# A gated mix of sliding-window and recurrent memory attention: tail products moved into the sliding branch's last block, and one ring of streamed weight slices for tail and steps

## The chip, the cores and the metric

The kernel runs on one core of one Trainium2 chip. The metric is device time in microseconds (us), the median over runs. Engines: PE (TensorE) multiplies, DVE (VectorE), ACT (ScalarE) and POOL (GpSimd) do the rest, SP (SyncE) only issues transfers; POOL issues some as well. "PEld" is PE loading weights. The granted clock is the share of PE's full clock that the chip allowed.

## The reference, cut to what matters

Two branches on the same input, mixed by a gate:

```
x = A_x; g = sigmoid(sum(x * gate_w))                    # one gate per token
# A: causal attention over a window of 256, 32 heads of 20, 2048 tokens, width 640
a = A(x, wqkv, wo)
# B: 64 segments of 32 tokens, 32 heads of 192, with 8 memory tokens ahead of each
mem = mem0
for s in range(64):
    h = concat([mem, x[32*s : 32*s+32]])                 # 40 tokens
    q, k, v = h @ Wq, h @ Wk, h @ Wv                     # 640 -> 32 x 192 each
    p = softmax(mask(q @ k.T * 192**-0.5))               # memory rows see all keys
    o = (p @ v) @ Wo                                     # 32 x 192 -> 640
    mem, b[s] = o[:8], o[8:]
out = g * a + (1 - g) * b
```

Branch B is serial: a segment's memory is an output of the segment before. `branch_A` therefore prepares the input for B as well.

## The kernel before, in words

Four stages follow each other.

1. **Sliding branch** (`branch_A`), 16 blocks of 128 queries, 32 heads each. A loop over n (block and head) emits, per pair of heads, scores by query (PSUM banks "s", L327), their row maximum on DVE (L357), and 22 heads later scores by key ("st") with the exponential on ACT (L387) and a mask on POOL (L395); eight heads after that come the values (L411). Between them stand units from a list: the next block's preparation (transposes, Q, K and V products in banks "m") and the projection of the block before (L435, L445). For the last block there is no next block to prepare. Transposed input goes to DRAM for branch B (`xa_dram`), and the last eight tokens of each segment into `xTb` (its *tail* tokens). A list `units` holds SP's work for branch B: 21 weight slices are packed into DRAM (`w_packed`) and 23 resident weight tiles are loaded (`early`). A unit is taken when n is divisible by a number that grows as the list gets shorter; what is left at the end is added without any condition.
2. **Tail.** The 24 tokens of a segment that are not its tail tokens go through the steps together with the 8 memory tokens, 32 columns at a time. The Q, K and V of the tail tokens depend on no memory, so they are made in advance for all segments, per group g of eight heads: `tail_qk` (L590; four blocks of six products, 20 matmuls each) and `tail_v` (L610), written to DRAM as `xbqk` and `xbv`. Q and K of group 0 are added at the end of the sliding branch, with banks "s"; the rest is `tail_projections`: V of group 0, the initial memory turned by PE (L640) and copied to `m0T`, Q and K of groups 1 to 3, V of groups 1 to 3. The remaining resident weights (`late`) are loaded on SP here. Streamed slices come through a ring `t_w` of three.
3. **Steps** (`branch_B`), 64 of them, in the order of the string `STEP`. q, k, v are products of the 32-column `hT` with weight slices (L775); scores (L847), softmax, transposed probabilities (L896), values (L921) and the output projection (L945) follow for each of four groups. The output projection ends a step: DVE writes its memory columns into the next `hT` (L956), and the next step's products wait for that. Of the weights, 21 slices a step are streamed from `w_packed` through a ring of five (L754 on SP); the others are resident. `last`, two o tiles of group 3, are loaded during step 0, four issues of 80 KB each (L532).
4. **Mix** (`mix_out`): gate and sum, to the output.

The order on each engine is fixed ahead by a planner (`Sched`). It keeps, per buffer tag, the rule that a buffer is written only after the users of the one that held its slot, gives each operation a duration and a latency, and takes the ready operation with the longest chain behind it. On PE it does that in the sliding branch only; in tail and steps PE keeps the order in which operations were made. SP and POOL execute their queues in the planned order: an issue that waits holds all behind it.

For the first step, `load_x(0)` brings `hT` from `xa_dram` on POOL (L732) and DVE copies `m0T` into it (L762); both belong to `branch_B`. The rings of tail and steps are separate pools, and the steps' pools take the memory that the tail's pools gave back:

```
shape = {"ts": (2, [P, P // MEM, 2, 12, MEM]), "w": (3, [P, WQ]), "m0": (1, [P, D])}   # tail
"w": (5, [P, WQ]), "hT": (1, [P, KT, SEG]), ...                                         # steps
early, late, last = weights.resident[:23], weights.resident[23:-2], weights.resident[-2:]
```

Of the kernel before, what the change touches and what calls it, by code (L numbers as in the profile page):

```python
# [139 lines left out]
def branch_A(tc, x, wqkv, wo, gate_w, spread_x, ga_dram, omg_dram, units, tail, W=256, HA=32):  # L140
# [13 lines left out]
    with ExitStack() as ctx:  # L154
# [307 lines left out]
        for _, u in prep_units(0):  # L462
            u()
        queue, credit, share = [], 0.0, 0.0
        job = lambda n: divmod(n, HA) if 0 <= n < HA * NB else None
        for n in range(HA * NB + LAG2):
            t, h = divmod(n, HA)
            if h == 0:
                if t + 1 < NB:
                    queue += prep_units(t + 1)  # L470
                credit, share = 0.0, sum(c for c, _ in queue) / (HA - 3)
            if n >= HA and units and n % max(1, HA * (NB - 2) // (len(units) + 1)) == 0:
                units.pop(0)(sc, [o for o in sc.ops[-8:] if o["eng"] == "PE"][-1:])
# [12 lines left out]
            while queue and credit > 0 and n % BURST == BURST - 1:  # L486
                c, u = queue.pop(0)
                credit -= c
                u()
        for u in units:  # L490
            u(sc, [])
        for _, u in queue:
            u()
        tail(sc)
        with tc.manual_schedule():
# [6 lines left out]
WQ, WO = 4 * 384, 2 * D  # L502
PARTS = {"q": KT, "k": KT, "v": KT, "o": 6}


# [69 lines left out]

def tail_qk(sc, nc, weights, xTb, xbqk, g, loads, after=(), tag="m"):

    HS = P // MEM
    ws = tail_weights(sc, nc, weights, g, "qk", loads)
    for t in range(xbqk.shape[2] // HS):  # L580
        st = sc.buf("ts")
        for n in range(6):
            kind, b4 = "qk"[n // 3], n % 3
            ps, use = sc.buf(tag), [ws[kind, g, kt] for kt in range(KT)]

            def f(ps=ps, use=use, b4=b4, t=t):
                for bb in range(4):
                    c = (4 * b4 + bb) * P
                    for kt in range(KT):
# [3 lines left out]
            evacuate(sc, nc, n, ps, st, lambda st=st, n=n, b4=b4: sc.tile(st)[:, :, n // 3, 4 * b4:4 * b4 + 4, :].rearrange("p s b t -> p b s t"),  # L593
                     lambda ps=ps: sc.tile(ps)[:].rearrange("p (b s t) -> p b s t", b=4, t=MEM))
        sc.op("POOL", 1000, lambda st=st, t=t: nc.gpsimd.dma_start(xbqk[g, :, t * HS:(t + 1) * HS].rearrange("p s k c -> p (s k c)"),
                                                                 sc.tile(st)[:].rearrange("p s k b t -> p (s k b t)")), reads=[st])


# [18 lines left out]

def tail_projections(tc, weights, xTb, xbqk, xbv, post, late, mem0, m0T, ident):

    nc = tc.nc  # L620
    with ExitStack() as ctx:
        shape = {"ts": (2, [P, P // MEM, 2, 12, MEM]), "w": (3, [P, WQ]), "m0": (1, [P, D])}
        pools = {t: ctx.enter_context(tc.tile_pool(name=f"t_{t}", bufs=n)) for t, (n, _) in shape.items()}
        pools["m"] = ctx.enter_context(tc.tile_pool(name="t_ps", bufs=8, space=bass.MemoryType.PSUM))

        def make(tag, n):
            if tag == "m":
                return pools[tag].tile([P, 512], FP32, name="t_psum", tag=tag)
            return pools[tag].tile(shape[tag][1], BF, name=f"t_{tag}", tag=tag)
        sc = Sched({"ts": 2, "w": 3, "m": 8, "m0": 1}, make)  # L630
        loads = {}
        for n, u in enumerate(late):
            loads[u] = sc.op("SP", 1300, lambda u=u: weights.load_resident(post, u, nc.sync), after=[loads[late[n - 1]]] if n else [])
        tail_v(sc, nc, weights, xTb, xbv, 0, loads)
        m0, tp = sc.buf("m0"), sc.buf("m")
        view = lambda: sc.tile(tp)[:].bitcast(BF)[:, 0:KT * MEM].rearrange("p (k t) -> p k t", k=KT)

        def turn_m0():
            for kt in range(KT):
                nc.tensor.transpose(view()[:, kt, :], sc.tile(m0)[0:MEM, kt * P:(kt + 1) * P], ident[0:MEM, 0:MEM])  # L640
        sc.op("DMA", 500, lambda: nc.gpsimd.dma_start(sc.tile(m0)[0:MEM], mem0), writes=[m0])
        sc.op("PE", 300, turn_m0, reads=[m0], writes=[tp], name=("m0",), mode=128)
        sc.op("DVE", dve_ns(40), lambda: nc.vector.tensor_copy(m0T[:], view()), reads=[tp])
        for g in range(1, 4):
            tail_qk(sc, nc, weights, xTb, xbqk, g, loads)
        for g in range(1, 4):
            tail_v(sc, nc, weights, xTb, xbv, g, loads)
        with tc.manual_schedule():
            sc.run()
# [4 lines left out]

KEPT = {"QT": (1, [P, 12 * L + 64 - L]), "Kz": (1, [P, 4, 2, L]), "Px": (1, [P, P])}

# [35 lines left out]

def branch_B(ctx, tc, xa_dram, xbqk, xbv, m0T, constants, weights, xo_dram, last):
    nc = tc.nc
# [5 lines left out]
    sb = {  # L700
        "w": (5, [P, WQ]), "hT": (1, [P, KT, SEG]), "tok": (2, [P, 384]), "vtok": (1, [P, 384]), "K02": (1, [P, 4, 2, L]),
        "PTm": (1, [P, 2, 4, L]), "PTx": (1, [P, 2, 4, L]), "OT": (1, [P, 3, 4, L]), "Pm": (1, [P, 4, SEG]),
        "xqk": (2, [P, 2, 12, MEM]), "xv": (1, [P, 384]), "oT": (1, [P, KT, SEG]),
    }
    ps = {"mm": 3, "tr": 2, "s": 2, "o": 1}
    pools = {t: ctx.enter_context(tc.tile_pool(name=f"b_{t}", bufs=n)) for t, (n, _) in sb.items()}
    pools |= {t: ctx.enter_context(tc.tile_pool(name=f"b_ps_{t}", bufs=n, space=bass.MemoryType.PSUM)) for t, n in ps.items()}
    stats = ctx.enter_context(tc.tile_pool(name="b_stats", bufs=3))
    sc = Sched({t: n for t, (n, _) in sb.items()} | {t: n for t, (n, _) in kept.items()} | ps)

    def tile_of(b, shape=None, dtype=BF, name=None):
        t = b["tag"]
        if b["tile"] is None:
            if t in kept:
                b["tile"] = still[t][b["n"] % kept[t][0]]
            elif t in sb:
                b["tile"] = pools[t].tile(sb[t][1], BF, name=f"t_{t}", tag=t)
            else:
                b["tile"] = pools[t].tile(shape, dtype, name=name or f"p_{t}", tag=t)
# [40 lines left out]

    hts = {0: load_x(0)}
    sc.op("DVE", dve(40), lambda: nc.vector.tensor_copy(tile_of(hts[0][0])[:, :, 0:MEM], m0T[:]), writes=[hts[0][0]], after=[hts[0][1]])  # L762
    made, tails, loads = {}, {}, {}
# [251 lines left out]
def kernel(  # L1015
# [32 lines left out]
    weights = Weights(nc, dram, B_Wq, B_Wk, B_Wv, B_Wo, streamed)  # L1048
    early, late, last = weights.resident[:23], weights.resident[23:-2], weights.resident[-2:]
    pre = ctx.enter_context(tc.tile_pool(name="b_pre", bufs=1))  # L1050
# [7 lines left out]
    with tc.tile_pool(name="b_xtail", bufs=1) as xtail:  # L1058
        xTb = xtail.tile([P, KT, nseg * MEM], BF, name="xTb")

        def spread_x(sc, qb, xT):
# [3 lines left out]
            for i in range(n):  # L1065
# [8 lines left out]
        branch_A(tc, x, A_wqkv, A_wo, gate_w, spread_x, ga_dram[:], omg_dram[:], units,  # L1074
                 lambda sc: tail_qk(sc, nc, weights, xTb, xbqk, 0, packs, xTb_ops[-1:], "s"))
        const = ctx.enter_context(tc.tile_pool(name="b_const", bufs=1, side="right"))
        constants = constants_B(nc, const)
        m0T = const.tile([P, KT, MEM], BF, name="m0T")
        post = ctx.enter_context(tc.tile_pool(name="b_post", bufs=1, side="right"))
        tail_projections(tc, weights, xTb, xbqk, xbv, post, late, mem0, m0T, constants[1])  # L1080

    with ExitStack() as inner:
        end = inner.enter_context(tc.tile_pool(name="b_end", bufs=1))
        branch_B(inner, tc, xa_dram, xbqk, xbv, m0T, constants, weights, xo_dram, {u: lambda u=u: weights.load_resident(end, u, nc.sync) for u in last})
    mix_out(tc, xo_dram, omg_dram[:], ga_dram[:], outf)
# [35 lines left out]
```

## Time and profile before

| | us |
|---|---|
| median of 7 runs | 2268.62 |
| lowest and highest run | 2260.5, 2283.53 |
| profiled execution, its time | 2268.62 |
| its span, first to last instruction | 2266.9 |

| stage of the profiled execution | from, to (us) | PE busy, us of stage | granted clock | DMA, GB/s |
|---|---|---|---|---|
| sliding branch to the first L590 | 0, 360 | 337.17 of 360 | 0.98 | 80 |
| L590 of group 0 and the branch's end | 360, 400.5 | 39.86 of 40.5 | 0.98 | 69 |
| tail | 400.5, 541 | 136.16 of 140.5 | 0.98 | 243 |
| step 0 | 541, 578 | 26.37 of 37 | 0.94 | 284 |
| steps 1 to 62 | 578, 2205.5 | 1496.80 of 1627.5 | 0.98 | 307 |
| step 63 and mix | 2205.5, 2267 | 35.18 of 61.5 | 0.72 | 246 |

"Busy" of PE is the time in which some matmul is under way; matmuls overlap, so a busy PE may still run at half clock. The chain of waits follows the work that ended last back to its releasers; the table of PE's waits counts the time in which PE stood still, by what ended it. The two can differ: the chain names a transfer even when PE had other work until just before it landed.

### The profile page before, as it was taken

How to read it: one execution, taken by the hardware profiler on the slowest of the kernel's cores; microseconds unless marked ns; L12 is line 12 of the kernel's file. 1: busy time of each engine (PE TensorE's matmuls, PEld its weight loads, DVE VectorE, ACT ScalarE, POOL GpSimd, SP SyncE). 2: the span in 40 equal slices, each digit the busy share in tenths (PEclk: the TensorE clock that was granted, in tenths of full speed). 3: DMA queues.
4: the chain of work that ended last, by engine and by line, in shares of the span. 5: the costliest groups of instructions: out<-in, count | busy, mean ns of one | idle time of the engine just before them, and what ended most of it. 6: DMA issues, size and time to landing. Idle time of an engine off the chain costs nothing.

```text
span 2266.9 us, 112856 instructions
## 1 busy us (share of the span) xinstructions
PE 2071.5 (91%) x49093; PEld 1508.1 (67%) x49093; DVE 1123.9 (50%) x3943; ACT 1055.8 (47%) x2385; POOL 693.6 (31%) x1998
## 2 busy tenths in 40 slices
PE   7999999998899899999999998999999999999995
PEld 5777767895666666666666666666666666666663
DVE  6988884223344444444444444444444444444444
ACT  4888885223343444444444444444444344444443
POOL 5555553002222222222222222222222222222220
PEclk9999998999999999999999999999999999999996
DMA  4221212668899998999999999999999898999997
GB/s 148 80 62 54 70 50 92 240 220 270 293 309 297 304 308 298 313 314 307 315 313 305 311 313 310 303 309 307 311 309 309 296 307 293 305 308 319 309 320 239
DMA packets 263841, 591.70 MB, mean 261 GB/s; under 512 B 54696, under 2 KB 71344, under 8 KB 263344
## 3 DMA queue, kind: packets, MB, share of 16 engines
q1 hardware_dynamic: 240096, 537.19, 71.1%
q0 software_dynamic: 18976, 43.03, 5.4%
q8 instruction: 384, 6.29, 1.1%
q10 hardware_dynamic: 4272, 4.26, 0.6%
q14 instruction: 113, 0.93, 0.1%
HBM read 554.98 MB, written 36.97 MB: 261 GB/s over the span
## 4 chain that ended last, share of the span: by engine, by line
PE 69%; DMA 22%; ACT 4%; issue 3%; SPq 1%; DVE 1%; POOL 0%; ACTq 0%; POOLq 0%; DVEq 0%
DMA t_w<-w_packed 18%; PE ps_o L945 12%; PE ps_k L775 9%; PE ps_q L775 9%; PE ps_v L775 7%; PE ps_pv L921 4%; PE p_m L282 4%; PE p_s L327 4%; PE t_psum L590 4%; PE tr_q L790 2%; PE tr_k L790 2%; PE p_o L411 2%; PE S_ps L847 2%; PE p_st L327 1%; ACT t_tok L780 1%
## 5 line engine op out<-in xcount | busy, mean ns | idle before, releaser
L775 PEld LDWEIGHTS <-t_hT 128*32 128x32 bf16 x15360 | 374.2, 97 | 284.3 <-issue 53.2
L945 PE MATMUL ps_o<-t_OT,w_o 128*128 128x40 bf16 x8960 | 329.2, 180 | 60.2 <-ACT t_OT L926 45.2
L945 PEld LDWEIGHTS <-w_o 128*128 128x128 bf16 x8960 | 281.5, 96 | 68.1 <-issue 58.6
L945 PE MATMUL ps_o<-t_OT,t_w 128*128 128x40 bf16 x6400 | 264.7, 180 | 21.6 <-DMA t_w<-w_packed 12.4
L357 DVE CUSTOM_DVE_ANT_0 a_junk<-p_s,a_mask 128x384 bf16<-128x384 f32 (+2 forms) x512 | 253.3, 528 | 41.0 <-PE p_st L327 28.0
L822 POOL COPY t_K<-t_xqk 128x64 bf16<-128x64 bf16 x256 | 60.8, 238 | 688.0 <-PE S_ps L847 682.5
L775 PE MATMUL ps_q<-w_q,t_hT 128*32 128x384 bf16 x4352 | 233.2, 338 | 24.7 <-DVE t_hT L956 20.7
L387 ACT ACTIVATE a_pt<-p_st 128x384 bf16<-128x384 f32 (+2 forms) x512 | 219.8, 474 | 42.3 <-PE p_st L327 32.6
L926 ACT CAST t_OT<-ps_pv 128x480 bf16<-128x480 f32 x256 | 143.2, 560 | 205.1 <-PE ps_pv L921 197.8
L945 PEld LDWEIGHTS <-t_w 128*128 128x128 bf16 x6400 | 207.9, 96 | 32.4 <-DMA t_w<-w_packed 24.2
L775 PE MATMUL ps_v<-w_v,t_hT 128*32 128x384 bf16 x4352 | 226.3, 330 | 2.4 <-issue 2.3
L857 DVE TENSOR_REDUCE sm_mx<-S_ps 128x4 f32<-128x160 f32 x256 | 82.5, 322 | 258.5 <-PE S_ps L847 258.5
L775 PE MATMUL ps_k<-w_k,t_hT 128*32 128x384 bf16 x3840 | 206.3, 334 | 0.0
L780 ACT CAST t_tok<-ps_q 128x384 bf16<-128x384 f32 x256 | 122.7, 479 | 150.7 <-PE ps_q L775 150.7
L395 POOL TENSOR_SCALAR_AFFINE_SELECT a_pt<-a_pt 128x512 bf16<-128x512 bf16 x240 | 148.0, 640 | 129.5 <-ACT a_pt L387 128.6
L813 DVE COPY t_K<-tr_k 128x256 bf16<-128x256 bf16 x256 | 74.9, 293 | 223.9 <-PE tr_k L790 223.3
L904 DVE TENSOR_TENSOR t_PTx<-PT_ps,mk_x 128x320 bf16<-128x320 f32 x256 | 124.3, 486 | 112.1 <-PE PT_ps L897 112.0
L780 ACT CAST t_vtok<-ps_v 128x384 bf16<-128x384 f32 x256 | 122.7, 479 | 113.6 <-PE ps_v L775 113.6
L780 ACT CAST t_tok<-ps_k 128x384 bf16<-128x384 f32 x256 | 122.7, 479 | 113.3 <-PE ps_k L775 110.6
L799 ACT COPY b_QT<-tr_q 128x384 bf16<-128x384 bf16 x256 | 123.0, 480 | 100.0 <-PE tr_q L790 99.7
L744 POOL DMA_DIRECT2D t_xqk<-xbqk x256 | 139.5, 545 | 83.2 <-POOL b_QT L803 38.8
L327 PE MATMUL p_st<-a_qa,a_k 64*128 64x128 bf16 x1440 | 147.2, 221 | 5.3 <-ACT a_pt L387 3.5
(145 smaller groups left out, 4044.0 us busy)
## 6 DMA issues: line engine op xcount, KB each, us to landing
t_w<-w_packed SPq DMA_DIRECT2D x714, 384.0 KB, 5.0
t_w<-w_packed SPq DMA_DIRECT2D x640, 320.0 KB, 4.6
t_xqk<-xbqk POOLq DMA_DIRECT2D x256, 48.0 KB, 4.5
xbqk<-t_ts POOLq DMA_DIRECT2D x12, 768.0 KB, 5.1
w_q<-in_B_Wq_dram SPq DMA_DIRECT2D x17, 384.0 KB, 4.5
w_v<-in_B_Wv_dram SPq DMA_DIRECT2D x17, 384.0 KB, 7.0
xbv<-t_ts POOLq DMA_DIRECT2D x16, 384.0 KB, 4.2
t_xv<-xbv POOLq DMA_DIRECT2D x64, 96.0 KB, 4.3
```

The source lines that it names most:

```text
L282: nc.tensor.matmul(view()[:, gg, :], lhsT=Wp[:, kt, 4 * g:4 * g + 4, :].rearrange("p h d -> p (h d)"), rhs=T(k["xT"])[:, kt, :], start=(kt ...
L327: nc.tensor.matmul(T(out)[:, i * P:(i + 1) * P], lhsT=b if keys_first else a, rhs=a if keys_first else b, start=True, stop=True, tile_posi ...
L357: sc.op("DVE", 135 + n / 0.96, lambda: nc.vector.tensor_tensor_reduce(out=T(junk)[:, 0:n], in0=T(s)[:, 0:n], in1=mask[:, NKB * P - n:], op ...
L387: sc.op("ACT", act_ns(n), lambda: nc.scalar.activation(out=T(pt)[:, h % 4, 0:n], in_=T(s)[:, 0:n], func=ACT.Exp), reads=[s], writes=[pt])
L395: nc.gpsimd.affine_select(out=v, in_=v, compare_op=op, fill=0.0, base=0, pattern=[[0, 4], [sign, P]], channel_multiplier=-sign)
L744: sc.op("DMA", 500, lambda: nc.gpsimd.dma_start(tile_of(qk)[:].rearrange("p i b t -> p (i b t)"), xbqk[g, :, s].rearrange("p i c -> p (i c ...
L775: nc.tensor.matmul(t[32 * j:32 * j + 32, 0:384], lhsT=tile_of(hT)[:, kt, :], rhs=w[:, j * 384:(j + 1) * 384], start=(kt == kts[0]), stop=( ...
L780: sc.op("ACT", act(384), lambda: nc.scalar.copy(tile_of(tok)[:], b["tile"][:, 0:384]), reads=[b], writes=[tok])
L799: nc.scalar.copy(dst, tq["tile"][:].rearrange("p b (j t) -> p b j t", t=SEG))
L904: nc.vector.tensor_tensor(out=tile_of(dst)[:], in0=PT["tile"][:, i, :, :].unsqueeze(2).to_broadcast([P, 2, 4, L]), in1=mk.unsqueeze(1).uns ...
L926: sc.op("ACT", act(480), lambda: nc.scalar.copy(tile_of(OT)[:].rearrange("p b j l -> p (b j l)"), o["tile"][:, 0:480]), reads=[o], writes= ...
L945: nc.tensor.matmul(t[:, dt * L:(dt + 1) * L], lhsT=w[:, r * D + dt * P:r * D + (dt + 1) * P], rhs=OT["tile"][:, b, i, :], start=(g == 0 an ...
```

## The change

Five things change:

- `tail_qk` becomes a generator that yields after each product. `branch_A` draws one product at each odd n from 485 (block 15, head 5) on; its bank tag is "m" while n is below 512, then "s".
- The spacing of `units` is computed once (`every`), and the list must be empty before the products begin.
- One ring of five slices, opened on the right side beside the constants, serves tail and steps. The initial memory is loaded into a buffer of this ring.
- `hT` becomes a kept tile among the constants. In the tail, POOL loads segment 0's `xa_dram` into it, and DVE copies the turned memory straight into its first columns; `m0T`, `load_x(0)` and its copy in `branch_B` go.
- `last` grows from two resident o tiles to four, and `late` shrinks by two.

```diff
@@ branch_A
-        queue, credit, share = [], 0.0, 0.0
+        queue, credit, share, fill = [], 0.0, 0.0, None
+        every = max(1, HA * (NB - 2) // (len(units) + 1))
...
-            if n >= HA and units and n % max(1, HA * (NB - 2) // (len(units) + 1)) == 0:
+            if n >= HA and units and n % every == 0:
                 units.pop(0)(sc, [o for o in sc.ops[-8:] if o["eng"] == "PE"][-1:])
...
-        for u in units:
-            u(sc, [])
+            if n > HA * (NB - 1) + 4 and n % BURST:
+                if fill is None:
+                    assert not units
+                    fill = tail(sc, lambda: "m" if n < HA * NB else "s")
+                next(fill, None)
         for _, u in queue:
             u()
-        tail(sc)
+        for _ in fill:
+            pass
@@ tail_qk
-            ps, use = sc.buf(tag), [ws[kind, g, kt] for kt in range(KT)]
+            ps, use = sc.buf(tag()), [ws[kind, g, kt] for kt in range(KT)]
...
+            if n < 5:
+                yield
         sc.op("POOL", 1000, lambda st=st, t=t: nc.gpsimd.dma_start(xbqk[g, :, t * HS:(t + 1) * HS]...
+        yield
@@ tail_projections
-        shape = {"ts": (2, [P, P // MEM, 2, 12, MEM]), "w": (3, [P, WQ]), "m0": (1, [P, D])}
+        shape = {"ts": (2, [P, P // MEM, 2, 12, MEM])}
+        pools["w"] = ring
-        sc = Sched({"ts": 2, "w": 3, "m": 8, "m0": 1}, make)
+        sc = Sched({"ts": 2, "w": RING, "m": 8}, make)
-        m0, tp = sc.buf("m0"), sc.buf("m")
+        m0, tp = sc.buf("w"), sc.buf("m")
-        sc.op("DVE", dve_ns(40), lambda: nc.vector.tensor_copy(m0T[:], view()), reads=[tp])
+        xl = sc.op("DMA", 500, lambda: nc.gpsimd.dma_start(hT[:].rearrange("p k t -> p (k t)"), x0))
+        sc.op("DVE", dve_ns(40), lambda: nc.vector.tensor_copy(hT[:, :, 0:MEM], view()), reads=[tp], after=[xl])
@@ KEPT
+RING = 5
-KEPT = {"QT": (1, [P, 12 * L + 64 - L]), "Kz": (1, [P, 4, 2, L]), "Px": (1, [P, P])}
+KEPT = {"QT": (1, [P, 12 * L + 64 - L]), "Kz": (1, [P, 4, 2, L]), "Px": (1, [P, P]), "hT": (1, [P, KT, SEG])}
@@ branch_B
-        "w": (5, [P, WQ]), "hT": (1, [P, KT, SEG]), "tok": (2, [P, 384]), ...
+        "tok": (2, [P, 384]), ...
+    pools["w"] = ring
-    hts = {0: load_x(0)}
-    sc.op("DVE", dve(40), lambda: nc.vector.tensor_copy(tile_of(hts[0][0])[:, :, 0:MEM], m0T[:]), writes=[hts[0][0]], after=[hts[0][1]])
+    hts = {0: (sc.buf("hT"), None)}
@@ kernel
-    early, late, last = weights.resident[:23], weights.resident[23:-2], weights.resident[-2:]
+    early, late, last = weights.resident[:23], weights.resident[23:-4], weights.resident[-4:]
...
+        ring = ctx.enter_context(tc.tile_pool(name="b_ring", bufs=RING, side="right"))
```

## The prediction

> **What bounds the kernel now.** I read the page's slices first, then the windows of the end of the sliding branch, of the tail and of the first recurrent step, then PE's waits in each, and the SP queue last. Slices:
>
> ```profile
> PE   7999999998899899999999998999999999999995
> DMA  4221212668899998999999999999999898999997
> ```
>
> PE is the bound nearly everywhere; the 64 recurrent steps (541 to about 2230 us) take most of the span. In them PE hardly waits for slices:
>
> ```profile
> PE ps_o L945 <- ACT t_OT L926: 43.1, 61, 0.7
> PE ps_q L775 <- DVE t_hT L956: 20.1, 61, 0.9
> PE ps_o L945 <- DMA t_w<-w_packed: 9.6, 26, 1.5
> ```
>
> These three waits (us in total, times, longest) cover 1,600 us. The steps are PE's own work plus short waits of the recurrence, 26.25 us each ((2205.5 - 577.97)/62, by the starts of L956). The change touches none of this, so what it wins or loses lies before 605 us. Three places there are not full. First, the end of the sliding branch (columns: stretch, PE busy, PEld, DVE, ACT, POOL, granted clock, DMA share, GB/s):
>
> ```profile
> 335.00:340.00 5.00, 4.74 (x93) 3.14 (x90) 3.73 (x16) 4.38 (x12) 1.87 (x6) 1.00 0.00 0
> 340.00:345.00 5.00, 3.78 (x77) 2.57 (x75) 4.54 (x19) 4.61 (x11) 2.76 (x6) 0.96 0.69 212
> 345.00:350.00 5.00, 4.38 (x64) 2.98 (x61) 4.58 (x20) 3.56 (x9) 2.85 (x6) 0.50 1.07 301
> 350.00:355.00 5.00, 4.69 (x69) 2.98 (x66) 3.96 (x15) 3.69 (x8) 2.52 (x5) 0.50 0.04 0
> 355.00:360.00 5.00, 3.80 (x69) 2.62 (x66) 3.35 (x15) 2.75 (x7) 1.67 (x3) 0.50 0.03 3
> 360.00:365.00 5.00, 5.00 (x72) 4.73 (x71) 1.53 (x5) 2.55 (x5) 2.44 (x6) 0.83 0.00 0
> ```
>
> With no next block to prepare, PE thins out, and from 345 us the granted clock is half. At 360 us the 24 segment-0 products (L590) begin, and PE is dense at full clock up to 400 us. Second, one stall in the tail:
>
> ```profile
> 441.00:442.00 1.00, 0.03 (x1) 0.00 (x0) 0.00 (x0) 0.43 (x1) 0.28 (x1) 1.00 0.35 37
> 444.00:445.00 1.00, 0.43 (x5) 0.43 (x6) 0.00 (x0) 0.00 (x0) 0.00 (x0) 0.50 1.01 320
> 450.00:451.00 1.00, 1.00 (x17) 1.00 (x16) 0.31 (x1) 0.00 (x0) 0.00 (x0) 0.77 1.05 421
> 474.00:475.00 1.00, 0.77 (x14) 0.60 (x12) 0.00 (x0) 0.59 (x1) 0.00 (x0) 1.00 1.01 359
> ```
>
> The chain names two waits for t_w here, 3.75 us at 440.78 and 3.78 us at 470.73. The windows show that only the first idles PE: 441 to 444.57 is empty and the clock is half until 450.5; at 474 PE loses 0.23 us. Third, the way into the first step, by PE's waits from 541 to 579 and SP's issues:
>
> ```profile
> PE ps_q L775 <- DVE t_hT L762: 3.0, 1, 3.0
> PE ps_k L775 <- DMA t_w<-w_packed: 2.7, 1, 2.7
> PE ps_o L945 <- DMA t_w<-w_packed: 2.3, 4, 1.1
> PE ps_o L945 <- DMA w_o<-in_B_Wo_dram: 1.9, 2, 1.4
> ...
> 544.71 14.53 SPq L754 DMA_DIRECT2D t_w<-w_packed  x13
> 559.29 3.35 SPq L532 DMA_DIRECT2D w_o<-in_B_Wo_dram  x4
> 562.75 7.68 SPq L754 DMA_DIRECT2D t_w<-w_packed  x8
> 570.48 3.15 SPq L532 DMA_DIRECT2D w_o<-in_B_Wo_dram  x4
> ```
>
> **The change, part by part.**
>
> *Products in the last block.* 24 products of 20 matmuls, about 1.12 us each (480 such take 26.88 us in the chain), are now made one at each odd n from 485. The first 14 (n up to 511) use banks "m" and may run beside block 15's scores; ten still need the "s" banks, as all 24 did. From 340 to 365 us PE did 3.78x0.96 + 4.38x0.50 + 4.69x0.50 + 3.80x0.50 + 5.00x0.83 = 14.2 us of work at full clock, so 10.8 us are free; 14 products (15.7 us) fill that. Behind it, up to 400 us, PE is full and only moves forward. Upper bound: -10.8. Lower: the clock stays at half and only the idle 3.35 us are used, at half rate, -1.7. A loss would need PE to stop longer for late casts than those 3.35 us; from 300 to 340 us, with as many casts between, it stopped 0.55 us, so I exclude it. The row nearest is the stage from 300 to 340 us, where the same score chain runs with preparation in its gaps: PE 19.7 of 20 at clock 1.00. I take four fifths, **-8.5**. [...] The trace has the clock fall just as PE thins out and return within 2 us of the dense products, so I follow the trace.
>
> The casts of the products move too: seven each of 0.69 us on DVE and 0.59 us on ACT into block 15. DVE is busy 16.4 of 20 there, ACT 14.6; with 4.8 and 4.1 more both stay under the 26 us that PE now needs. A cast that waits for a late product holds the maxima (DVE) and exponentials (ACT) behind it, and the four stores of 0.55 us on POOL hold the affine selects; PE's scores would wait for these. That is the fifth I leave out. The last ten products cover the final projection as before.
>
> *Loads spread evenly.* Eleven of SP's 44 packing and loading units came at n 442 to 534, three at 7.4 to 12.4 us; now all lie at n 36 to 423, beside dense PE work with DMA 0.1 to 0.3 busy. SP's x loads of a later block queue behind at most four more issues of 0.5 to 0.6 us, one block ahead of need. Cost 0; -1 to +1 us (the early three may leave the first x load sooner; without the lead each issue costs its 0.5 us).
>
> *Ring of five in the tail.* Slice q2_4 needed k1_3's slot and so the end of group 1. With five, and m0 as the first tenant (free at about 414), it goes out at once; q3_4, k3_4 and the three v slices then wait for slots a whole group ahead of use. Won: idle 0.97 + 1 + 1 + 0.57 = 3.54, the half clock (0.43 + 5.0) x 0.5 + 0.23 = 2.95, and 0.23 at 474: **-6.7**. [...] SP still blocks at ring loads in the tail, with late weights queued behind; after group 2's end it needs about 6 us for v issues and, at 0.60 us an issue and four a tile, 10 x 2.4 = 24 us for w_o, inside the 66 us left. The x0 load and the copy into hT hide there too: POOL and DVE are under a third busy.
>
> *Way into step 0.* hT is ready, and slices for steps can be issued into slots of q3_4, k3_4, v1_4 and v2_4 before the tail ends. Gone: 3.0 for hT, 2.7 for k0_4, and the half clock from 548 to 553.2 (about 1.9). New: PE waits for the last casts, 0.6. And the small buffers now lie, by my count of sizes, on the tail's staging buffer (four w_o tiles below them), whose last store xbv was issued at 541.57 and landed at 544.7. POOL issues that store and then waits for it before t_xqk, which in the old kernel it issued at 542.10; the K and Q copies behind it on POOL then let s0 start near 548.4 instead of 553.03: **-4.6**. If there is no such overlap, -6; if xqk lands later still, -2.
>
> *Four w_o in step 0.* Each is four issues; SP put the two old ones where the ring was full: after 13 and after 21 slices. The second was issued from 570.48 to 573.02 and landed at 577.14, and PE waited for it. Two more behind each other in that place cost 2 x 2.54 = **+5.1**, with next-step slices queued behind them on SP. If they find earlier gaps, 0; if slices are starved too, +9. The tail wins nothing from their leaving, since there they were covered.
>
> Sum: -8.5 + 0 - 6.7 - 4.6 + 5.1 = -14.7. The profiled execution took 2268.62 us (span 2266.9 and 1.7 around it), which is also the median of the seven: 2254.
>
> **The rivals.**
> 1. *The sliding gain fails.* The casts hold back DVE and ACT in their fixed order, and the clock stays at half: -1.7 instead of -8.5, so -7.9, about 2261. For it: DVE is over 80% busy in that block. Against: it ran at 88% with preparation between, and PE was full.
> 2. *The w_o loads find gaps.* With slices ahead, they are issued before PE comes to them: 0 instead of +5.1, with the o slices' 2.3 us mostly gone: -21.5, about 2247. Against: SP is at most five slices ahead of PE and issues w_o only when the ring is full.
> 3. *Slower: the planner's order of steady steps changes.* Step 0 has other operations now, and the order of SP's slices could settle into another repeating pattern. Slices cost PE 22 us in 61 steps now (9.6 + 6.6 + 6.1), 0.37 per step. From 0.23 us more per step the 14.7 are eaten; at +0.5 per step, 64 steps give +32 - 14.7, about 2286. Against: lists, ring size and durations of each step are the same.
> 4. *It doesn't do what it says*: the stall at 441 stays because SP blocks earlier on another load: -8, about 2261.
>
> **How the numbers follow.** My forecast 0.50, rival 1 0.14, rival 2 0.17, rival 3 0.07, rival 4 0.06, and 0.06 for rivals 1 and 4 together (about 2267). Half a per cent, about what a measurement of this kernel can tell from no change, is 11.3 us: faster below 2257.3. The seven runs lie 23 us apart and the steps' own half-clock spells vary, so the forecast's own error is about 7 us: seven tenths of its 0.50 (0.35), nearly all of rival 2 and a third of 1 and 4 are faster, together 0.58. Slower is rival 3 and a little more, 0.09; the rest, 0.33, is within half a per cent. The range runs from rival 2 with error to rivals 1 and 4 with error: 2242 to 2267.
>
> **What would show it.** PE's clock at 1.00 through the last block and the tail starting near 392 us; no empty window in the tail and 133.5 us of dense L590 and L610; the first step's q products within 1 us of the last cast; 16 L532 issues in step 0 and a PE wait for w_o of several us at its end; step period 26.2 to 26.3. It is wrong if the clock still halves in the last block, if t_w waits stay in the tail, or if the step period moves.

## The result, and the profile after

| | before | after |
|---|---|---|
| median, us | 2272.45 (61 runs, 2253.12 to 2284.47) | 2263.66 (24 runs, 2247.26 to 2279.55) |
| ratio | | 0.9971, 95% interval 0.9953 to 0.9989 |
| span of the profiled execution | 2266.9 | 2258.9 |

The change makes the kernel faster by 0.29%, some 6.6 us; 14.7 us were forecast (2254). The forecast started from the median of seven runs, 2268.62 us; over 61 runs the kernel before takes 3.8 us more, so of the 9.7 us between 2254 and 2263.66 that much lies in the starting point. Timed twice more beside other kernels, the change gave 0.9964 (0.9942 to 0.9986) and 0.9986 (0.9965 to 1.0007). The mean of the three ratios is 0.9974, or 6 us. Ratios are reckoned from the fast runs alone (none over 1.5% above the fastest of its kernel), so they are not quite the quotients of the medians.

The page's slices after:

```profile
PE   7999999998889999999999999999989999998995
DMA  3322211677889999999989999999999999999987
```

PE is as full as before. In the DMA row, the loads of the sliding branch lie a little more evenly over the first six slices.

PE's waits from 541 to 2205 us, which answer to the three shown of before:

```profile
PE ps_o L957 <- ACT t_OT L938: 43.8, 62, 0.7
PE ps_q L787 <- DVE b_hT L968: 23.2, 63, 1.7
PE ps_o L957 <- DMA t_w<-w_packed: 14.8, 34, 1.4
```

The same waits in nearly the same sizes (this stretch takes in step 0, that of before did not): the steady steps were not changed, 26.196 us each against 26.255.

The end of the sliding branch, in windows (stretch, PE, PEld, DVE, ACT, POOL, granted clock, DMA share, GB/s):

```profile
340.00:345.00 5.00, 5.00 (x99) 4.54 (x100) 4.06 (x14) 2.76 (x7) 2.70 (x6) 1.00 0.28 34
345.00:350.00 5.00, 3.39 (x68) 2.76 (x66) 1.79 (x6) 1.36 (x3) 0.06 (x1) 1.00 0.03 3
350.00:355.00 5.00, 4.19 (x45) 3.41 (x45) 2.69 (x9) 2.33 (x5) 1.22 (x2) 0.61 0.00 0
355.00:360.00 5.00, 5.00 (x83) 4.49 (x84) 2.69 (x9) 2.30 (x6) 2.01 (x3) 0.71 0.40 156
360.00:365.00 5.00, 5.00 (x110) 4.21 (x105) 3.27 (x12) 3.88 (x9) 1.80 (x4) 1.00 0.02 8
...
390.00:395.00 5.00, 3.48 (x69) 3.10 (x69) 0.37 (x1) 2.38 (x5) 2.85 (x5) 1.00 0.06 14
395.00:400.00 5.00, 3.46 (x17) 1.45 (x13) 0.75 (x2) 1.08 (x2) 0.02 (x1) 0.55 0.39 157
```

From 340 to 345 us the products fill PE as hoped. Then two holes: one at 345 to 355 us, after which the clock is low until 358 us, and one at the branch's very end, where before was full:

```profile
390.00:395.00 5.00, 5.00 (x120) 5.00 (x117) 1.70 (x4) 1.77 (x3) 0.55 (x1) 1.00 0.49 193
395.00:400.00 5.00, 4.86 (x73) 4.15 (x71) 1.73 (x3) 1.38 (x3) 0.54 (x1) 1.00 0.12 38
```

(the kernel before). The timeline of PE after shows what stands in the second hole:

```profile
392.85 0.22 PE L596 MATMUL p_s<-xTb,a_w 128*128 128x128 bf16 x1
394.59 0.46 PE L411 MATMUL p_o<-a_v,a_pt 128*128 128x21 bf16 x12 [1.52 <-POOL a_pt L395]
394.90 0.27 PE L435 MATMUL p_m<-a_ident,a_an 128*128 128x128 bf16 x2
395.93 0.50 PE L435 MATMUL p_m<-a_ident,a_an 128*128 128x128 bf16 x3 [0.75 <-DVE a_an L419]
397.21 2.85 PE L445 MATMUL p_m<-woA,a_aT 128*128 128x512 bf16 x10 [0.78 <-ACT a_aT L437]
400.57 1.78 PE L619 MATMUL t_psum<-w_v,xTb 128*128 128x384 bf16 x5 [0.51 <-DVE a_ga L452]
```

The last of the 24 products ends at 393 us. Behind it the last mask, values, transposes, projection and gate follow each other with nothing beside them, 7.5 us, the projection's 2.85 us at half clock (the same ten matmuls took 1.52 us at a clock of 1.00 in the kernel before). In the kernel before, the last product ended only 0.7 us before the tail, so products lay beside this chain to its end. The tail starts at 400.57 us; it did before at 400.53.

Tail windows that answer to those of before:

```profile
441.00:442.00 1.00, 1.00 (x22) 1.00 (x20) 0.30 (x1) 0.27 (x1) 0.00 (x0) 1.00 0.00 0
444.00:445.00 1.00, 1.00 (x22) 1.00 (x20) 0.00 (x0) 0.59 (x1) 0.00 (x0) 1.00 1.02 344
474.00:475.00 1.00, 1.00 (x22) 1.00 (x20) 0.69 (x1) 0.00 (x0) 0.00 (x0) 1.00 0.98 390
```

The stall and its half clock are gone. The way into step 0, by PE's waits from 530 to 578 us and by SP's timeline:

```profile
PE ps_o L957 <- DMA w_o<-in_B_Wo_dram: 6.3, 5, 3.4
PE ps_o L957 <- DMA t_w<-w_packed: 1.6, 2, 1.4
PE ps_q L787 <- ACT t_ts L577: 0.6, 1, 0.6
...
548.94 2.41 SPq L538 DMA_DIRECT2D w_o<-in_B_Wo_dram  x4
551.46 8.10 SPq L767 DMA_DIRECT2D t_w<-w_packed  x8
559.61 8.34 SPq L538 DMA_DIRECT2D w_o<-in_B_Wo_dram  x12
```

The first q products wait 0.6 us for the last cast, and the four w_o tiles hold SP at the end of the step: twelve issues in 8.34 us while PE waits 6.3 us.

One profiled execution isn't enough here: the kernel before, run again, gave a span of 2271.7 us, and its stages moved by up to 7 us. So every run below is read by stages, all in us. "Branch's end": from the last gate matmul (L263, at 336 to 340) to the first matmul of the tail. "Half clock": the spells at a granted clock of 0.5 that began after 344 us and before the tail. "Tail": from there to its last matmul. "Step 0": from the last matmul of the tail to the first copy into `hT`. "Steps": the 62 periods after. "End": step 63 and the mix.

| kernel | branch's end | half clock | tail | step 0 | steps | end |
|---|---|---|---|---|---|---|
| before | 64.5 | 17.1 | 139.9 | 37.6 | 1627.8 | 61.1 |
| before again (e5) | 63.1 | 13.7 | 139.3 | 34.1 | 1635.1 | 61.4 |
| after | 64.6 | 13.7 | 133.4 | 36.6 | 1624.1 | 64.2 |
| after again (e1) | 60.2 | 6.8 | 133.8 | 37.3 | 1636.8 | 62.4 |
| after, third (e11) | 61.7 | 6.8 | 133.5 | 36.0 | 1627.7 | 60.9 |
| no products in block 15 (e2) | 66.5 | 20.5 | 132.5 | 36.0 | 1633.4 | 62.3 |
| products alone (e3) | 58.5 | 0 | 138.6 | 36.4 | 1630.3 | 60.5 |
| five held back (e4) | 59.1 | 3.4 | 132.5 | 37.6 | 1631.8 | 62.3 |
| ring and step 0 alone (e6) | 65.6 | 17.1 | 132.5 | 36.8 | 1632.2 | 62.4 |
| w_o early (e7) | 62.2 | 6.8 | 133.7 | 38.2 | 1629.3 | 60.9 |
| products in quarters, w_o early (e8) | 64.2 | 6.8 | 132.5 | 38.5 | 1620.6 | 61.7 |
| packed w_o (e9) | 60.6 | 6.8 | 133.7 | 34.0 | 1636.5 | 63.6 |
| five held, packed w_o (e10) | 64.0 | 10.2 | 132.6 | 32.3 | 1635.8 | 61.3 |
| five held again (e12) | 60.1 | 6.8 | 132.6 | 37.6 | 1648.0 | 60.7 |

The table has one profiled execution of each. The steps alone scatter over 27 us, without any pattern by kernel. This is why a part worth 5 us hardly shows in a median of some twenty runs, while the stage shows it.

### The profile page after: what moved, and what is told of

Read it like the earlier page. It is cut to its first block, busy times and chain, and to the rows that moved or that the text cites. A ratio compares the mean times of both kernels' runs of the same rounds, so it can differ in the third digit from the quotient of the medians.

```text
span 2258.9 us, 112850 instructions
## 1 busy us (share of the span) xinstructions
PE 2061.4 (91%) x49093; PEld 1501.6 (66%) x49093; DVE 1127.4 (50%) x3942; ACT 1054.6 (47%) x2385; POOL 694.2 (31%) x1999
## 4 chain that ended last, share of the span: by engine, by line
PE 70%; DMA 21%; ACT 4%; issue 3%; POOL 1%; DVE 1%; SPq 1%; ACTq 0%; DVEq 0%; POOLq 0%
DMA t_w<-w_packed 17%; PE ps_o L957 12%; PE ps_k L787 8%; PE ps_q L787 8%; PE ps_v L787 7%; PE ps_pv L933 4%; PE p_m L282 4%; PE p_s L327 4%; PE t_psum L596 4%; PE t_psum L619 2%; PE tr_q L802 2%; PE tr_k L802 2%; PE p_o L411 2%; DMA b_hT<-xa_dram 2%; PE S_ps L859 2%
## 5 line engine op out<-in xcount | busy, mean ns | idle before, releaser
L787 PEld LDWEIGHTS <-b_hT 128*32 128x32 bf16 x15360 | 374.7, 97 | 275.9 <-issue 42.4
L957 PEld LDWEIGHTS <-w_o 128*128 128x128 bf16 x8960 | 281.3, 96 | 71.4 <-issue 61.1
L834 POOL COPY t_K<-t_xqk 128x64 bf16<-128x64 bf16 x256 | 60.9, 238 | 677.7 <-PE S_ps L859 674.0
L787 PE MATMUL ps_q<-w_q,b_hT 128*32 128x384 bf16 x4352 | 229.5, 334 | 24.4 <-DVE b_hT L968 23.2
L787 PE MATMUL ps_v<-w_v,b_hT 128*32 128x384 bf16 x4352 | 227.1, 330 | 3.4 <-issue 3.3
L787 PE MATMUL ps_k<-w_k,b_hT 128*32 128x384 bf16 x3840 | 205.2, 332 | 0.1
L875 ACT ACTIVATE S_ps<-S_ps 128x160 f32<-128x160 f32 x256 | 74.5, 291 | 155.8 <-DVE S_ps L872 147.4
```

The source lines that it names most:

```text
L787: nc.tensor.matmul(t[32 * j:32 * j + 32, 0:384], lhsT=tile_of(hT)[:, kt, :], rhs=w[:, j * 384:(j + 1) * 384], start=(kt == kts[0]), stop=( ...
L957: nc.tensor.matmul(t[:, dt * L:(dt + 1) * L], lhsT=w[:, r * D + dt * P:r * D + (dt + 1) * P], rhs=OT["tile"][:, b, i, :], start=(g == 0 an ...
```

## The experiments

My theory from the first profile: the tail won what was forecast, the way into step 0 came out even, and what is missing was to come from the sliding branch, whose final chain now lies bare. The rivals: one unlucky profile, a loss in the steps, and a loss by the loads' new places.

**e1, the changed kernel once more.** No edit.

> The changed kernel once more, unchanged, for a second profile and as the yardstick of this group. In its first profile PE stood still for 2.4 us at 347.7 to 352 us, the clock fell to half for 6.8 us behind it, and from 393 to 400.6 us PE had only the last projection's chain. Theory A (the gain of the sliding branch is lost in the order that the planner fixed: bare chain at the end): the tail begins near 395 us if the stop at 348 us was chance, near 400 us if it belongs to the program; the bare chain of some 7 us is there in both. Ratio to the kernel before 0.997, which is -6 to -7 us. Theory B (the spread won its 8.5 us in most executions and only this profile shows a stop): tail begins at 392 to 393 us.

Measured: 2261.81 us, ratio 0.9964 (0.9942 to 0.9986). Branch's end 60.2 us against 64.6, with the clock low only at the very end, so the first profile was partly unlucky. The bare end is there again:

```profile
390.00:395.00 5.00, 2.73 (x50) 2.18 (x47) 0.75 (x2) 1.56 (x3) 2.86 (x5) 1.00 0.15 53
395.00:400.00 5.00, 3.31 (x15) 1.56 (x15) 0.35 (x1) 1.38 (x2) 0.00 (x0) 0.52 0.29 118
```

**e2, no products in block 15.** All 24 come after the loop, as before; the rest of the change stays.

```diff
-            if n > HA * (NB - 1) + 4 and n % BURST:
-                ...
-                next(fill, None)
...
-        for _ in fill:
+        assert not units
+        for _ in tail(sc, lambda: "s"):
             pass
```

> The changed kernel with its 24 products put back behind the sliding branch's list, banks s, as in the kernel before; ring, hT and the four o tiles stay. Theory A (spread is worth about nothing, all of the gain is the ring's): within 2 us of the changed kernel, ratio to before 0.996 to 0.998, tail beginning near 400.5 us. Rival (the forecast: the spread is worth 8.5 us and something later gives it back): 6 to 9 us slower than the changed kernel, ratio 1.000. Third (the stop at 348 us is chance and the spread is worth about 5 us): 4 to 6 us slower than the changed kernel.

Measured: 2266.95 us, ratio 1.0002 (0.998 to 1.0024). The windows are those of the kernel before, clock and all:

```profile
345.00:350.00 5.00, 3.82 (x79) 2.66 (x76) 4.30 (x19) 4.07 (x10) 2.96 (x6) 0.82 0.20 4
350.00:355.00 5.00, 2.73 (x36) 1.86 (x36) 2.83 (x11) 2.47 (x7) 1.68 (x4) 0.50 0.03 3
```

Branch's end 66.5 us with 20.5 us at half clock, and a full PE from 390 to 405:

```profile
395.00:400.00 5.00, 5.00 (x120) 5.00 (x118) 1.16 (x4) 2.03 (x4) 0.55 (x1) 1.00 0.45 180
400.00:405.00 5.00, 4.95 (x78) 4.41 (x77) 2.28 (x4) 1.18 (x2) 0.00 (x0) 1.00 0.14 49
```

So most of the half clock of block 15 belongs to the missing filler, and the bare end to the spread products.

**e3, products alone.** `branch_A` and `tail_qk` of the changed kernel; ring, hT and `last` as before.

> The kernel before with the spread products and the even loads alone; the ring of three, m0T and two o tiles stay. Theory A: ratio 0.998 to 1.001, tail beginning near 400 us. Rival (the forecast): -8.5 us, ratio 0.996, tail near 392 us. Third (stop by chance): -4 to -6 us, ratio 0.998.

Measured: 2265.47 us, ratio 0.9987 (0.9971 to 1.0003). Branch's end 58.5 us, the shortest of all. The clock did not fall, though PE was as thin at the end as in the changed kernel:

```profile
350.00:355.00 5.00, 4.37 (x70) 3.12 (x65) 3.21 (x10) 2.29 (x6) 1.22 (x2) 1.00 0.00 0
390.00:395.00 5.00, 2.57 (x43) 1.87 (x40) 0.75 (x2) 2.26 (x4) 1.79 (x3) 1.00 0.28 116
395.00:400.00 5.00, 4.19 (x27) 2.57 (x29) 1.16 (x3) 1.17 (x2) 0.53 (x1) 1.00 0.21 77
```

With the ring of three the tail keeps its wait, so the ring is what removes it:

```profile
PE t_psum L595 <- DMA t_w<-w_packed: 3.5, 2, 3.1
```

**e4 and e12, five products held back.** The last five of the 24 wait for the last values but one, so that the planner must put them beside the final chain.

```diff
+                if drawn < 19:
+                    next(fill, None)
+                    drawn += 1
...
+        extra += [o for o in sc.ops if o["name"] == ("pv",)][-2:][:1]
...
-            sc.op("PE", 20 * 56, f, ..., after=list(after) + [u[1] for u in use], ...
+            sc.op("PE", 20 * 56, f, ..., after=list(after) + list(extra) + [u[1] for u in use], ...
```

> The changed kernel, but the last five of the 24 products may start only after the last but one group of values, so that they lie in the final projection's chain. Theory A: PE has work from 390 us to the end, the clock stays full, the tail begins 3 to 5 us earlier than in the changed kernel of this group; ratio to before 0.995. Rival (the end of the branch is not what costs: the chain from the last scores is as long in any order, or the products held back were needed before): 0 to 2 us slower than the changed kernel.

> The kernel with five products kept back once more, to see whether its 2257 of the first time holds (with packed o tiles the same five gave 2263.65). If the five are worth what the branch's end showed the first time (tail 59.1 us after the gate, against 60 to 65 in the changed kernel): ratio to the kernel before 0.993 to 0.996 again and a half clock of at most 3.4 us at the branch's end. If the first time was scatter: ratio 0.997 to 0.998, 2262 to 2264, as the changed kernel.

Measured: 2256.99 us, ratio 0.9951 (0.993 to 0.9971), and the second time 2259.66 us, 0.9959 (0.9929 to 0.9988). In e4 the last ten microseconds are filled, and the thin place moves ahead of them:

```profile
385.00:390.00 5.00, 4.18 (x57) 3.24 (x57) 0.00 (x0) 3.43 (x8) 3.59 (x7) 0.75 0.27 105
390.00:395.00 5.00, 5.00 (x91) 5.00 (x89) 2.04 (x4) 0.82 (x2) 1.16 (x3) 0.91 0.05 14
395.00:400.00 5.00, 4.35 (x42) 2.93 (x40) 0.91 (x2) 2.27 (x5) 0.54 (x1) 1.00 0.39 157
```

Branch's end 59.1 and 60.1 us, against 64.6, 60.2 and 61.7 in the changed kernel. These are the two lowest ratios of all, and both intervals lie below 1: it beats the kernel before. It is also the version I would keep against the changed kernel; the intervals still overlap that one's, and e10, which holds back the same five, comes out no better (0.998), so its lead over it is likely, not shown. The profiled execution of e12 took 2279.66 us; what it has above the median lies in the steps (1648.0).

**e5, the kernel before, one run for its profile.**

> The kernel before, unchanged, for a second profile: in the group so far every profile had short half-clock spells between 50 and 280 us that the first profiles of both kernels had not, so its stages are needed from the same group. Both theories: from the last gate product (L263) to the first tail product 64 to 66 us with the clock at half for 17 us or more, tail 140 us, step 0 with the handover 37 to 38 us.

Measured: 2273.4 us, stages in the table. The way into step 0 took 34.1 us here and 37.6 the first time: this stage varies by itself by as much as I had argued about.

**e6, ring and step 0 alone.** The changed kernel with the old `branch_A` loop and spacing.

> The kernel before with the ring of five, hT and four o tiles alone; loads and products of the sliding branch as in the kernel before. Theory C (the tail's 6.5 us arrive, handover and step 0 come out even, the spread is worth 4 to 6 us more): tail 133 us, stretch before it 64 to 66 us, ratio 0.997 with an interval of about 0.002 on either side. Rival (what the ring wins is given back in steps or at the end, by about 2 us each): tail 133 us, but the steps from the first L968 to the last at 1632 us or more and 62 to 64 us behind them where the kernel before has 61; ratio 0.999 to 1.000.

Measured: 2269.67 us, ratio 1.0007 (0.9986 to 1.0029), a miss: the tail is 132.5 us, 6.8 to 7.4 shorter than before, and the median doesn't show it. Its profile has the other stages on the long side (branch's end 65.6, end 62.4, steps in the middle). Loads at their old places (e6) and spread (e2) give the same branch's end within 1 us and the same tail, so no cost of the loads can be seen.

**e7, w_o early.** The four w_o loads get the first rank on SP once the 22nd PE operation of the steps is done.

```diff
-            loads[u] = sc.op("SP", 1300, last.pop(u), after=[...][8:9])
+            loads[u] = sc.op("SP", 1300, last.pop(u), after=[...][21:22])
+            loads[u]["first"] = 1e7
```

> The changed kernel, with the four o tiles issued on SP right behind the sixth or seventh slice of step 0, by a priority in the planner, and not where the ring is full. Theory (the w_o term of the sum is real: twelve issues in a row, 559.6 to 567.3 us, and PE waiting until 569.8): handover and step 0 take 30 to 33 us in place of 36.5 to 37.3, PE waits for w_o under 1 us, ratio to the changed kernel 0.997 to 0.998. Rival (slices starve behind the ten us of w_o issues early in the step, or the recurrence bounds step 0 anyway): 36 us or more, with waits for t_w in q, k or v products.

Measured: 2264.58 us, ratio 0.9996 (0.9972 to 1.0021). Step 0 took 38.2 us, no less. PE's waits and SP's timeline say why:

```profile
PE ps_q L788 <- DMA t_w<-w_packed: 8.3, 1, 8.3
...
536.27 6.90 SPq L768 DMA_DIRECT2D t_w<-w_packed  x3
543.53 11.22 SPq L538 DMA_DIRECT2D w_o<-in_B_Wo_dram  x16
```

The wait for w_o is gone, and one of 8.3 us for a slice that stands behind the sixteen issues has come. Moved to this place, the cost stays: the slices now wait for SP.

**e8, products in quarters.** On top of e7's edit, each product is made of four operations of five matmuls, so that scores can go between.

> As e7, and each of the 24 products as four operations of five matmuls for the planner, so that it fills smaller gaps and blocks the scores for 0.28 us and not 1.12. Theory (whole products delay the score chain: query scores of block 15 end at 372 us in every spread kernel and at 360 in the kernel before, and fillers are used up at 393): query scores end by 366 us, the fillers reach into the last projection, and the stretch from the last gate product to the tail is 55 to 57 us in place of 60. Rival (more switches of PE's tiling cost what the finer filling wins): 59 to 62 us.

Measured: 2269.77 us, ratio 1.0013 (0.9992 to 1.0034). The fillers do reach to the end of the branch, and the last scores by query come somewhat earlier (31 us after the gate; 33 to 38 in the kernels with whole products drawn early). Branch's end is 64.2 us all the same, two more than in e7, which differs from it in nothing else. The whole stage of e1 and of e8, with the same 6.8 us at half clock in both, shows where they go:

```profile
339.10:399.40 60.30, 54.32 (x1000) 44.52 (x1003) 30.43 (x99) 36.63 (x81) 24.10 (x44) 0.96 0.19 61
338.40:402.70 64.30, 59.43 (x1005) 47.38 (x1003) 31.05 (x99) 37.71 (x81) 23.54 (x43) 0.95 0.14 48
```

PE is idle for 4.9 us instead of 6.0, but busy for 59.4 instead of 54.3, and for 3.6 to 5.1 more than in the four kernels with whole products and as much half clock (54.3 to 55.8). That is the outcome that the rival named; no run shows whether its reason, PE's switches, is the right one. The result speaks against finer pieces, and leaves open what the size of a product costs the scores.

**e9 and e10, packed w_o.** The four tiles are also packed into free slots of `w_packed` in the sliding branch, and each is loaded in step 0 by one issue of 320 KB; e10 holds five products back as well. **e11** is the changed kernel a third time, beside them.

```diff
+    units += [lambda sc, after, u=u: sc.op("SP", 1300, lambda: weights.copy(u, whole[u], nc.sync), after=after) for u in last]
...
+        t = weights.tiles[u] = pool.tile([P, WO], BF, name="w_%s%d%d" % u)
+        nc.sync.dma_start(t[:], whole[u])
```

> The changed kernel, except that the four o tiles of step 0 are also packed into free slots of w_packed during the sliding branch (four more SP units there, each four issues), so that each is then loaded in step 0 by one issue of 320 KB instead of four of 80 KB. Theory A (the term 'Four w_o in step 0' is SP's own issue time: 16 issues of 0.6 us, the last 12 of them 8.34 us in one piece while PE waits 6.3 us for w_o): SP's share falls to about 4 x 0.3 us, the wait for w_o to under 2 us, step 0 from 36.5 and 37.3 us to 30 to 32, and the whole by 5 to 6 us: about 2257 at the median, ratio to the kernel before near 0.994. Rival B (the transfers are bound by bandwidth, 1.28 MB beside a ring already at 0.8 of the DMA engines): the wait moves from w_o to t_w, as when the same issues were put earlier, and step 0 stays at 35 to 38 us. Rival C: the four extra units in the sliding branch hold SP's x loads there and cost what step 0 wins; then the sliding branch ends over 3 us later than 397 to 400.

> The packed o tiles together with the five products kept back for the end of the sliding branch. If the two parts add: branch end as with five products kept (tail starts 59 to 60 us after the gate), step 0 at 30 to 32 us as in the packed kernel, together 5 to 6 us below 2257, so about 2251, ratio 0.9925. If they do not add (step 0 at 35 us or more, or the branch back at 63 to 65 us), about 2257, ratio 0.995.

> The changed kernel once more, beside the two packed ones: 2262 to 2264 at the median, ratio 0.996 to 0.997; step 0 at 36.5 to 37.3 us; the sliding branch's end 60 to 65 us after the gate.

Measured: e9 2265.04 us, 0.9988 (0.9973 to 1.0004); e10 2263.65 us, 0.998 (0.9959 to 1.0001); e11 2264.34 us, 0.9986 (0.9965 to 1.0007). In the median nothing is won. In the stage, step 0 takes 34.0 and 32.3 us against 36.6, 37.3 and 36.0 (mean 36.6), so 2.6 and 4.3 less of the 5 to 6 expected. PE's waits and SP in e9:

```profile
PE ps_o L957 <- DMA w_o<-w_packed: 4.4, 2, 3.1
PE ps_o L957 <- DMA t_w<-w_packed: 1.5, 1, 1.5
...
549.06 9.18 SPq L767 DMA_DIRECT2D t_w<-w_packed  x8
558.28 2.28 SPq L1072 DMA_DIRECT2D w_o<-w_packed  x3
```

SP needs 2.28 us for three tiles instead of 8.34, but they still go out after the slices ahead of them and PE waits 4.4 us for their landing. These three took 6.1 us each from issue to landing (median), the twelve issues of 80 KB in the profile after 2.4 us. So issue time is a part of what the four tiles cost; whether the rest is their late place in the queue or the longer landing, no run tells. The wait for slices stayed at 1.5 us and the branch ended no later, so rivals B and C are not what is missing. e10's branch did not end at 59 to 60 us: PE stopped once for 3.0 us at 353 us, which the last section comes to.

## Why the prediction was right or wrong

The direction was right, by cause as well as by sign; the size was not. By stages, with means over the kernels that have the part and those that don't:

| step of the prediction | forecast | measured | from |
|---|---|---|---|
| Products in the last block | -8.5 | -3.6 | branch's end 61.3 (six kernels with spread whole products, none held) against 64.9 (four without) |
| Loads spread evenly | 0 | 0 | e2 against e6 |
| Ring of five in the tail | -6.7 | -6.2 | tail 133.0 (eleven kernels) against 139.3 (three) |
| Way into step 0 | -4.6 | -4.1 | last matmul of the tail to the first of s0 (step 0's scores of group 0, `S_ps`): 7.9 (seven kernels with the new step 0, w_o loads unaltered) against 11.9 (three) |
| Four w_o in step 0 | +5.1 | +4.9 | from there to the first copy into `hT`: 29.0 (the same seven) against 24.1 (three) |
| step 63 and mix | not foreseen | +1.1 | 62.1 (eleven) against 61.0 (three) |

The sum is -7.9 us, against -8.8 between the medians of the first timing and 6 us by the mean of the three ratios. Each stage is one reading per kernel: the -3.6 is sure to some 2.5 us either way (from the scatter within the two groups), which still leaves out the -8.5. The steps, 1632.4 us on the mean of the eleven kernels with the ring and 1631.1 of the three without, are left out, since they scatter over 27 us.

**The step that failed is "Products in the last block".** I took four fifths of the 10.8 us that PE had free between 340 and 365 us, and wrote: "Behind it, up to 400 us, PE is full and only moves forward", and "The last ten products cover the final projection as before." Both sentences are wrong. Drawn early, the products are used up early, and behind the last scores by key a chain of masks, values, transposes, projection and gate then stands without them. In the four kernels without early products the last scores by key come 50.5 us after the gate, on the mean, and 14.5 us of full PE follow. In the six with them they come at 52.9 us, so the scores did not move forward at all (those by query come eleven us later), and the stretch behind them shrinks only to 8.4 us. In the profile after, the products ran out at 393.0 us, 7.5 us before the end. Two single windows over the whole stage, of after and of e2, show that PE is no less idle for it:

```profile
336.00:400.60 64.60, 58.25 (x1005) 46.94 (x1003) 30.51 (x99) 36.55 (x81) 24.10 (x44) 0.91 0.17 57
339.80:406.30 66.50, 60.33 (x999) 50.23 (x1003) 30.70 (x99) 37.63 (x81) 23.40 (x43) 0.85 0.14 46
```

PE is idle for 64.60 - 58.25 = 6.4 us after, and for 6.2 in e2. Over all kernels it is 5.9 us with the spread (4.7 to 6.4 in six) and 4.6 without (3.7 to 6.2 in four). In the last ten us before the tail it is 3.3 to 4.0 us in each of the six and 0.7 in each of the four; ahead of that, 2.2 and 3.9 on the mean. So the filler saved 1.7 us in the gaps and laid 3.0 bare at the end. With five products held back the last ten us are idle for only 0.6 to 0.7 us, in e4, e12 and e10 alike. Over the whole stage PE is idle for 4.3 and 3.8 us in e4 and e12, on the mean 2.1 us less than in the three profiles of the changed kernel, and their branch's end is 2.6 us shorter; in e10, with its stop of 3.0 us, it is 6.7 us, and nothing is won.

What was won is clock. Over the thirteen kernels of the table apart from e8, the branch's end is close to a straight line in the time at half clock:

- none: 58.5 (e3); 3.4: 59.1 (e4); 6.8: 60.1 to 62.2 (five kernels); 10.2: 64.0 (e10)
- 13.7: 64.6 and 63.1; 17.1: 64.5 and 65.6; 20.5: 66.5

A fit gives 58.3 us plus 0.40 us for each us at half clock, with or without the spread. Without it the half clock took 17.1 us on the mean of four kernels, with it 6.8 of six. In the tail of the kernel before, PE started a matmul every 107 ns at a granted clock of 0.50 (445 to 450 us) and every 56 ns at 1.00 (451 to 456), so at about half the rate. By that estimate 10.2 us at half clock are 5.1 us of work at full clock; less the 1.3 us of idle time that were added, 3.8 are left, about the 3.6 measured. In the forecast's own terms: of its 10.8 us, some 7.4 were clock, of which 5.1 came, and 3.4 were idle time, of which nothing came and 1.3 were added. So the products do lift the clock inside block 15, and part of that is given back at the bare end, where the clock fell in five of the six kernels with spread whole products and none held back. e3, with filler in the gaps and no half clock, and e2 and e6, without filler and with 20.5 and 17.1 us of it, show that the low clock of block 15 came with PE thinning out; no wait in that stage was longer than 1.8 us in e2 (the nine of its costliest group come to 3.6) and 0.7 us in e6.

**The ring** did in the tail what was forecast, to half a microsecond: no wait for t_w in any tail with five slots, and the wait back in e3 with three. That the half clock after the stall is part of its worth was right too. The whole times do not bear it out alone, though. e2 and e6 have the ring and the new step 0 without early products; the stages (-6.2, -4.1, +4.9, +1.1) let one expect a ratio of 0.998, and they gave 1.0002 and 1.0007. Of the missing 5 us, two lie in their branch's end (66.0 us on the mean, 63.8 in the two profiles of the kernel before); the rest shows in no stage beyond its scatter and stays open. For the same reason the whole times cannot price the early products: between these two kernels and the changed one (0.9974) lie some 7 us, give or take four or five, which would fit the 8.5 as well as the 3.6. It is the stages that decide.

**The way into step 0 and the four w_o** came out as worked, each by itself: s0 starts 4.1 us sooner after the tail, for 4.6 forecast, and the rest of step 0 takes 4.9 us more, for 5.1. xbv's landing still sets t_xqk, SP puts four issues after 13 slices and twelve after 21, and PE waits 6.3 us for w_o. Packing gives back 2.8 us (e9) and 4.6 us (e10) of that second part. Rival 2 is out: the loads found no gap, and e7, which puts them first, starves the slices.

**Rival 3**, a new order of the steady steps, did not come about: 26.196, 26.400 and 26.253 us a step after, 26.255 and 26.373 before, and the same waits. **Rival 4** is out with the tail's windows. **Rival 1** comes nearest: the sliding gain fails by more than half, and the time by it, 2261, lies nearer to 2263.66 than my 2254; but its reason, casts that hold DVE and ACT, is not what the traces show first: DVE is less busy in the windows from 345 to 355 us (1.79 and 2.69 of 5 us) than before (4.58 and 3.96), and the holes are those of the final chain and of stops of PE itself. The time came near it by luck: the clock, which rival 1 leaves at half, did rise.

**Open:** the microsecond more in step 63 and mix. Its scatter (60.7 to 64.2 with the ring, 60.5 to 61.4 without) is as large as the difference, and no run takes it apart.

## What to carry to other kernels

Before work is moved into a gap, look at what it covered where it stood: filler that is drawn early leaves the chain that ends the stage bare, and then the gap has only moved. Try to keep back as much filler as that chain is long; here that filled the end in all three kernels that did it, and its worth in the whole time is likely, not shown. A load that no step waits for in the old place can have a price in its issues on the queue: here sixteen of some 0.6 us cost the step about the same in the two places where SP put them, and merging them into four gave back between half and nearly all. And where the steps scatter by 27 us, compare stages over all runs that share the part, not one pair of profiles, and say where the whole time does not confirm them.

## What the hardware showed that I had not expected

- **The half clock came in portions.** Each spell at a granted clock of 0.5 in these traces, but for the one that the kernel's end cuts off, lasted 3.41 us or a multiple: in the kernel before thirteen of 3.41, four of 6.83 and one of 17.07 us, in the profile after eleven of 3.41 and three of 6.83. At the branch's end they come to the 3.4 to 20.5 us of the table, and the same thin stretch brought one or not: PE busy 2.57 of 5 us from 390 to 395 left the clock at 1.00 in e3, 2.73 of 5 brought it down in e1 (0.52 from 395 to 400). In the steps there were 6 to 17 spells an execution, 27 to 68 us together. Steps with 31 us of it took 1620.6 and 1627.7 us, those with 68 us 1648.0; a fit over the fourteen profiles gives 0.34 us for each us at half clock, with a correlation of 0.66. So somewhat under half of this scatter goes with the spells; which is the cause of which, no run takes apart.
- **PE stopped with nothing to wait for.** In nine of the ten profiles with spread products PE stood still for 0.3 to 3.0 us in one piece between 347 and 356 us, and the profile names no releaser ("issue"); two such rows, of the profile after and of e10 (PE's timeline):

```profile
349.18 0.33 PE L596 MATMUL p_m<-xTb,w_k 128*128 128x128 bf16 x3 [1.09 <-issue]
...
356.13 0.26 PE L327 MATMUL p_st<-a_qa,a_k 64*128 64x128 bf16 x1 [3.04 <-issue]
```

  Without early products it is 0.15 us in e2, nothing in e6 and in the kernel before run again, and 0.86 us at 356 us in the kernel before. In the profile after, in e10 and in e11 (0.3 us) the clock is low behind it; in e1, e4, e7 and e12, with 1.1 to 1.6 us, it is not. In eight of the nine profiles the DMA queue of the instructions moves a block of 16 KB during the stop: in the profile after from 348.97 to 351.33 us, where PE stood still from 348.09 to 349.18; in e10 it is under way from 354.70 to 356.24 us, and PE goes on at 356.13. But in e9 the block starts only 0.7 us after the stop is over, and in e6 and e8 there is such a block near 352 us and no stop. What PE lacks there, its instructions or something that the trace has no event for, is open.
